# The second feed-forward layer of two tiles as a Strassen product, with blocks of two tiles that reach across batches

## The chip, the cores and the metric

The kernel runs on one core of a Trainium2 chip. The core has five engines that run side by side and wait for each other by semaphores: TensorE (matmul; in the profile PE, its weight loads PEld), VectorE (DVE), ScalarE (ACT), GpSimd (POOL) and SyncE (SP), whose queue issues nearly all of the DMA transfers. Each engine works through its instructions in the order in which the program wrote them. The metric is the device time in microseconds of one execution. The kernel before took a median of 1633.8 us in three runs (1633.7 to 1633.95).

## The reference

The computation has two stages. The first is attention in which each query keeps only its 32 largest scores; the second is a feed-forward layer with an ELU between two matrix products. All of it is in float32 on the chip (the weights arrive as float64 and are turned into float32 by the kernel).

```python
B, H, S, D = (8, 8, 576, 64)
scores = q @ k.transpose(0, 1, 3, 2) / sqrt(D)
kth = np.partition(scores, -32, axis=-1)[..., -32:-31]
scores = np.where(scores >= kth, scores, -1e9)
attn = exp(scores - max); attn /= sum(attn) + 1e-9
x = (attn @ v).transpose(0, 2, 1, 3).reshape(4608, 512)
h = x @ w_in                       # 512 x 2048
g = np.where(h > 0, h, exp(min(h, 0)) - 1)
out = g @ w_out                    # 2048 x 512
```

## The kernel before

**Tiles and steps.** Each batch has 576 queries: four tiles of 128 and a remainder of 64. The remainders of two batches, an even one and the odd one behind it, share one tile, so there are 36 tiles of 128 tokens for the feed-forward layer. A step is one tile and one pair of heads; there are 144 steps, 18 for each batch (`steps`, lines 578 to 616). Within a batch the tiles go in groups: (0,1), (2,3) and the remainder (first in odd batches, last in even ones); batch 0 takes its tiles singly.

**What a step does.** The main loop (lines 681 to 713) is software-pipelined over four steps. At step n it writes down: the score matmuls of step n+2 (`scores`, line 320), whose results ScalarE copies to `sc`; the value product of a finished group (`attend`, line 432; `avps`, its 20 matmuls run over the columns of all tiles of the group, then a ScalarE copy to `xT`); the four passes of `select` of step n on VectorE (line 342; row maxima of eight at a time and their replacement); the two halves of `mask` of step n-1 (line 367: a tiny subtraction on GpSimd, the gap, then two ScalarE activations, the second the exponential); the transposes of step n-2 on TensorE (`turn`, line 407); and `normalise` of step n-1 on GpSimd (line 390: five tiny operations and two over 576 columns). Batch 0 and 1 also carry the decoding of the weights.

**The feed-forward layer.** When a block (one, two or three tiles) has all its attention, `ffn_pieces` (line 499) appends its work to the list `ffn`. A piece `hidden(f)` (line 504) multiplies 128 of the 2048 inner columns: 4 matmuls for which the weights are a slice of `w_in` and the moving operand is `xT` of all tiles of the block (256 columns for two tiles, 384 for three). ScalarE takes the positive and the negative part out of the accumulator and applies the exponential; the last addition, a gate (`close_gates`, line 483), goes to GpSimd, in the early steps and the last block to VectorE. The result, `gT`, lies in two tiles of 8 inner blocks each. A piece `project(s, part)` (line 545) is a quarter of the second layer of one tile s: 4 matmuls with a 128x128 slice of `gT` as weights and 512 columns of `w_out` as moving operand. After the fourth part ScalarE copies the sum to `osb` and SyncE stores it. In this float32 kernel the profile shows each matmul as two instructions.

**The order.** The order on TensorE, VectorE, ScalarE and GpSimd is written out by hand (`manual_schedule`). Four times a step, `feed` (line 639) decides how many pieces are written there. It has a price for each piece (`HIDDEN`, `PROJECT`, lines 20 and 21) and a list `due` that says by which step how much work must be placed, so that each block's work is spread evenly until the next block is ready. What is left after the last step is written at the end, in one go (line 714).

**Transfers.** `load_halves` (line 223) loads one pair of heads of k and q in 8 transfers, `load_v` (line 255) loads v; the table `plan` (line 629) says how many steps ahead of the batch. All of them, and the output stores, go through SyncE's queue.

## Time and profile before

| | us |
|---|---|
| median of three runs | 1633.8 |
| the profiled execution, device time | 1633.17 |
| its span, first to last instruction | 1631.4 |
| TensorE busy (8276 matmuls) | 1569.5 |
| VectorE busy | 1454.4 |
| ScalarE busy | 1174.6 |
| GpSimd busy | 711.6 |
| TensorE in the second layer (line 551) | 522.5 |
| TensorE in the first layer (line 523) | 542.9 |

The mean granted TensorE clock was 0.988. In the lines of the profile, `ops` is the accumulator of the second layer, `hps` that of the first, `scps` the scores, `eps` the transposes and `avps` the value product. `L551` is line 551 of the kernel. A group's line gives: line, engine, operation, output <- inputs, shapes, count | busy us, mean ns of one | idle time of the engine before them and what ended it. A busy TensorE counts a matmul from its start to its modelled end, so that neighbours overlap; the chain of work that ended last gives the time from one start to the next.

### The profile page before, as it was taken

The page shows a single profiled execution, that of the slowest core. Times are in us where ns is not written, and L with a number is a line of the kernel's source. Part 1 is how long each engine was busy: PE and PEld are TensorE (multiplying, and loading weights), DVE is VectorE, ACT ScalarE, POOL GpSimd, SP SyncE. Part 2 cuts the span into 40 slices and gives each one's busy share as a digit, 9 for nine tenths or more (in the row PEclk, how much of TensorE's full clock was granted, in tenths as well). Part 3 has the DMA queues.
Part 4 walks back from the last instruction along what each step waited for, and adds up shares of the span by engine and source line. Part 5 has one row for each costly group of instructions (what it writes and reads, how often), then busy time and mean ns, then how long its engine had stood idle before and what let it go on. Part 6 is the DMA issues. An engine that isn't in the chain of part 4 may idle for free.

```text
span 1631.4 us, 25301 instructions
## 1 busy us (share of the span) xinstructions
PE 1569.5 (96%) x8276; PEld 1004.7 (62%) x8276; DVE 1454.4 (89%) x2980; ACT 1174.6 (72%) x2369; POOL 711.6 (44%) x1535
## 2 busy tenths in 40 slices
PE   4789999999999999999999999999999999999999
PEld 2477666766665757555566666655557575755564
DVE  7899999999999999999999699999999599998000
ACT  6987777877776868778577786868668695958521
POOL 4983345444443444444344443535435353534300
PEclk9779999999999999999999999999999999999999
DMA  8521310012100310022000200012100201000000
GB/s 243 187 79 36 65 37 1 7 22 45 43 1 19 54 37 7 7 40 46 23 8 15 55 21 25 1 28 45 36 14 1 43 1 36 1 13 1 7 14 13
DMA packets 188035, 56.17 MB, mean 34 GB/s; under 512 B 178176, under 2 KB 179200, under 8 KB 187904
## 3 DMA queue, kind: packets, MB, share of 16 engines
q1 hardware_dynamic: 186704, 54.26, 14.1%
q8 instruction: 66, 1.08, 0.3%
q14 instruction: 65, 0.53, 0.1%
q10 hardware_dynamic: 1200, 0.30, 0.1%
HBM read 45.09 MB, written 9.44 MB: 33 GB/s over the span
## 4 chain that ended last, share of the span: by engine, by line
PE 74%; ACT 14%; DVE 5%; POOL 3%; issue 1%; SPq 1%; DMA 1%; ACTq 0%; DVEq 0%; POOLq 0%
PE ops L551 29%; PE hps L523 22%; PE avps L448 10%; PE scps L329 7%; PE eps L422 5%; ACT sc L386 3%; DVE wk L356 2%; ACT sc L385 2%; ACT et L423 2%; DVE m L363 2%; ACT n L542 1%; ACT n L533 1%; ACT n L538 1%; ACT gT L536 1%; POOL sc L403 1%
## 5 line engine op out<-in xcount | busy, mean ns | idle before, releaser
L363 DVE MAX8 m<-wk 128x8 f32<-128x576 f32 x864 | 611.2, 751 | 0.3 <-POOL den L384 0.3
L523 PE MATMUL hps<-xT,w_in 128*128 128x256 f32 (+2 forms) x2432 | 542.9, 373 | 0.0
L551 PE MATMUL ops<-w_out,gT 128*128 128x512 f32 x1152 | 522.5, 598 | 0.0
L523 PEld LDWEIGHTS hps<-xT,w_in 128*128 128x128 f32 x2432 | 404.9, 192 | 97.4 <-issue 25.4
L356 DVE MATCH_REPLACE8 wk<-m,wk 128x576 f32<-128x576 f32 x576 | 424.5, 747 | 0.0
L551 PEld LDWEIGHTS ops<-w_out,gT 128*128 128x128 f32 x1152 | 208.6, 190 | 231.7 <-issue 230.6
L396 POOL TENSOR_SCALAR dene<-den 128x2 f32<-128x2 f32 x144 | 32.5, 225 | 693.1 <-ACT sc L386 692.5
L386 ACT ACTIVATE sc<-sc,den 128x576 f32<-128x576 f32 x288 | 223.4, 776 | 66.1 <-POOL den L384 44.4
L385 ACT ACTIVATE sc<-sc,m 128x576 f32<-128x576 f32 x288 | 225.0, 781 | 9.6 <-DVE m L363 9.5
L337 ACT ACTIVATE sc<-scps 128x576 f32<-128x576 f32 x288 | 170.9, 646 | 77.8 <-PE scps L329 77.8
L448 PE MATMUL avps<-et,vT 128*64 128x256 f32 (+2 forms) x2080 | 205.6, 328 | 20.1 <-ACT et L423 19.7
L329 PE MATMUL scps<-kqT 64*128 64x288 f32 (+1 forms) x1280 | 199.9, 443 | 25.1 <-ACT kqT L305 12.6
L349 DVE MAX8 m<-sc 128x8 f32<-128x576 f32 x288 | 202.6, 747 | 20.6 <-ACT sc L337 20.6
L403 POOL TENSOR_SCALAR sc<-sc,rec 128x576 f32<-128x576 f32 x288 | 213.5, 751 | 14.9
L423 ACT COPY et<-eps 128x512 f32<-128x512 f32 x288 | 164.6, 571 | 66.2 <-PE eps L422 66.2
L356 DVE MATCH_REPLACE8 wk<-m,sc 128x576 f32<-128x576 f32 x288 | 212.2, 746 | 0.0
L448 PEld LDWEIGHTS avps<-et,vT 128*64 128x64 f32 x2080 | 128.0, 141 | 101.0 <-ACT et L423 34.2
L422 PEld LDWEIGHTS eps<-ident,sc 128*128 128x128 f32 x1152 | 143.4, 143 | 72.4 <-issue 53.9
L493 POOL TENSOR_TENSOR gT<-n,gT 128x512 f32<-128x512 f32 (+1 forms) x120 | 166.2, 1385 | 38.0 <-ACT n L542 38.0
L422 PE MATMUL eps<-ident,sc 128*128 128x128 f32 x1152 | 174.1, 277 | 0.1
L329 PEld LDWEIGHTS scps<-kqT 64*128 64x128 f32 (+1 forms) x1280 | 107.0, 182 | 102.5 <-issue 46.2
L533 ACT ACTIVATE n<-hps 128x512 f32<-128x512 f32 (+1 forms) x156 | 87.0, 558 | 58.0 <-PE hps L523 57.1
(45 smaller groups left out, 988.5 us busy)
## 6 DMA issues: line engine op xcount, KB each, us to landing
raw<-in_moe_w_in_dram SPq DMA_DIRECT2D x16, 512.0 KB, 4.9
vT<-in_v_dram SPq DMA_DIRECT2D x64, 128.0 KB, 2.4
raw<-in_moe_w_out_dram SPq DMA_DIRECT2D x16, 512.0 KB, 3.8
out_dram<-osb SPq DMA_DIRECT2D x32, 256.0 KB, 2.0
kin<-in_k_dram SPq DMA_DIRECT2D x112, 72.0 KB, 2.4
qin<-in_q_dram SPq DMA_DIRECT2D x112, 72.0 KB, 2.5
kin<-in_k_dram SPq DMA_DIRECT2D x8, 128.0 KB, 4.7
vT<-in_v_dram SPq DMA_DIRECT2D x64, 16.0 KB, 2.2
```

Source lines behind the costliest of these rows:

```text
L329: nc.tensor.matmul(wide[i][rows, half, 0:HS], kq[part, q0 : q0 + u.t.ql], kq[part, k0 : k0 + HS], start=True, stop=True,)
L349: nc.vector.max(found[i], cur[i])
L356: nc.vector.match_replace(wk[i], found[i], cur[i], TAKEN)
L363: nc.vector.max(found[i], cur[i])
L385: nc.scalar.activation(sc, sc, AF.Prelu, scale=-1.0, bias=low, alpha=1.0 / STEEP)
L386: nc.scalar.activation(sc, sc, AF.Exp, scale=-STEEP, bias=gap, accum_out=u.den[:, i : i + 1])
L403: nc.gpsimd.tensor_scalar(u.sc[:, i, :], u.sc[:, i, :], rec[:, i : i + 1], 1.0, ALU.mult, ALU.mult)
L422: nc.tensor.transpose(ps[:, c * P : (c + 1) * P], sc[:, c0 : c0 + P], ident[:])
L423: nc.scalar.copy(g.et[:, chunks, u.at, :], ps[:, 0 : n * P].rearrange("p (c q) -> p c q", c=n),)
L448: nc.tensor.matmul(ps[i * D : (i + 1) * D, cols], vt[:, 2 * J + i if c == J else i * J + c, :], w, start=(c == 0), stop=(c == J),)
L523: nc.tensor.matmul(blk.h[:, f % bank, :], w_in[:, i, f * P : (f + 1) * P], blk.xT[:, i, 0:n_tok], start=(i == 0), stop=(i == NC - 1),)
L551: nc.tensor.matmul(blk.o[:], blk.gT[f // NG][:, f % NG, s * P : (s + 1) * P], w_out[:, f, :], start=(f == 0), stop=(f == NF - 1),)
```

## The change

The second layer of a block of two tiles is the product of a 256 x 2048 matrix with a 2048 x 512 one. Cut into halves in each direction, with a11, a12, a21, a22 for the quarters of `gT` (tile, half of the inner columns) and b11 to b22 for those of `w_out`, it is eight products of quarters. The changed kernel forms it with seven, in Winograd's form of Strassen's scheme:

- four differences of quarters of `w_out` (t1 = b12 - b11, t2 = b22 - t1, t4 = b21 - t2, t3 = b22 - b12) are made once, on GpSimd, in four steps at the start of batch 1 (`differences`), and stored to DRAM (`scratch`), in 16 pieces. They are read back for each block through six buffers of 256 KB, four pieces for each of the four products that use them (`stream`, on SyncE's queue, issued when the piece before has been used);
- four sums of quarters of `gT` per block are made in place by GpSimd, 128 x 1024 elements each, between the products;
- each product is 8 matmuls over 256 columns; ScalarE copies its result out, and seven sums of 128 x 256 on GpSimd put the four quarters of the output together. The two output tiles are stored after products 5 and 6.

Blocks of three tiles are gone. The first five blocks are single tiles, then the tiles in the order in which they finish are taken two by two, across batches; one single tile remains at the end. So that a pair always finishes together, batches 3, 4 and 7 go through their tiles as (0), (1,2), (3). With the first group of a batch single, batch 4 has its own loading plan. `xT` of the early single blocks has two buffers instead of three, the output tile two instead of one, and the price list of the planner counts seven products.

```diff
-HIDDEN = {1: 1.1, 2: 1.85, 3: 2.7}
+HIDDEN = {1: 1.1, 2: 1.85}
...
-    T = 3 * P
+    T = 2 * P
+    W = dm // 2
+    TF, TB = 2, 6
+    QT = NG // TF
...
-    xpool = pool("x", 3)
-    opool = pool("o", 1)
+    xpool = pool("x", 2)
+    opool = pool("o", 2)
+    scratch = pool("scratch", 1, space=bass.MemoryType.DRAM)
...
+        late["e"] = ctx.enter_context(tc.tile_pool(name="e", bufs=2))
+        late["t"] = ctx.enter_context(tc.tile_pool(name="t", bufs=TB))
...
+        def quarter(s, h):
+            return blk.gT[h][:, :, s * P : (s + 1) * P]
+
+        def combine(dst, x, y, op):
+            nc.gpsimd.tensor_tensor(dst, x, y, op)
+
+        def emit(s):
+            for t in blk.tiles[s]:
+                p0 = t.cols.start - s * P
+                nc.sync.dma_start(out[t.rows, :], blk.o[s][p0 : p0 + t.ql, :])
+
+        def product(j):
+            left, right = slice(0, W), slice(W, dm)
+            while blk.after:
+                blk.after.pop(0)()
+            if j == 7:
+                return
+            if j == 0:
+                close_gates(upto=(blk.number, NF - 1))
+                blk.o = [opool.tile([P, dm], FP32, tag="osb", name="osb") for _ in range(2)]
+                blk.e = [late["e"].tile([P, W], FP32, tag="e", name="e") for _ in range(2)]
+            a11, a12 = quarter(0, 0), quarter(0, 1)
+            a21, a22 = quarter(1, 0), quarter(1, 1)
+            c11, c12 = blk.o[0][:, left], blk.o[0][:, right]
+            c21, c22 = blk.o[1][:, left], blk.o[1][:, right]
+            e0, e1 = blk.e[0][:], blk.e[1][:]
+            x, name, dst, after = (
+                (a11, "b11", c11, [(a21, a21, a22, ALU.add)]),
+                (a12, "b21", c12, [(a11, a21, a11, ALU.subtract)]),
+                (a21, "t1", c22, [(a12, a12, a11, ALU.subtract)]),
+                (a22, "t4", e0, [(a21, a22, a11, ALU.subtract)]),
+                (a11, "t2", c21, [(c21, c21, c11, ALU.add), (c11, c11, c12, ALU.add)]),
+                (a12, "b22", c12, [(c12, c12, c21, ALU.add), (c12, c12, c22, ALU.add)]),
+                (a21, "t3", e1, [
+                    (c21, c21, e1, ALU.add), (c22, c22, c21, ALU.add),
+                    (c21, c21, e0, ALU.add),
+                ]),
+            )[j]
+            if j == 0:
+                combine(*after.pop())
+            sums = ps_f.tile([P, dm], FP32, tag="f", name="ops")[:, left]
+            for f in range(NG):
+                if name[0] == "b":
+                    w = w_out[:, NG * (name[1] == "2") + f, right if name[2] == "2" else left]
+                else:
+                    if f % TF == 0:
+                        t = streamed.pop(0)
+                    w = t[:, f % TF, :]
+                nc.tensor.matmul(sums, x[:, f, :], w, start=f == 0, stop=f == NG - 1)
+                if name[0] == "t" and f % TF == TF - 1:
+                    stream()
+            if 0 < j < 4:
+                combine(*after.pop())
+            nc.scalar.copy(dst, sums)
+            blk.after += [lambda x=x: combine(*x) for x in after]
+            if j > 4:
+                blk.after.append(lambda: emit(j - 5))
...
+        if blk.slots == 2:
+            return layer + [
+                (PROJECT * (j < 7), behind, lambda j=j: product(j), blk.number)
+                for j in range(8)
+            ]
...
+    def stream():
+        k = ahead_of[0]
+        ahead_of[0] += 1
+        if k >= 4 * QT * sum(x.slots == 2 for x in blocks):
+            return
+        t = late["t"].tile([P, TF, W], FP32, tag="t", name="tw")
+        src = kept[names[k // QT % 4], k % QT]
+        nc.sync.dma_start(t[:], src[:].rearrange("p (f n) -> p f n", f=TF))
+        streamed.append(t)
...
+    def differences(q):
...
+        for name, x, y in (
+            ("t1", b12, b11), ("t2", b22, "t1"), ("t4", b21, "t2"), ("t3", b22, b12),
+        ):
+            t = late["t"].tile([P, TF, W], FP32, tag="t", name="tw")
...
+            nc.gpsimd.tensor_tensor(t[:], x, y, ALU.subtract)
...
+            nc.sync.dma_start(
+                kept[name, q][:].rearrange("p (f n) -> p f n", f=TF), t[:]
+            )
...
     for b in range(B):
-        if b % 2 == 0:
...
+        if b == 0:
+            order = [(0,), (1,), (2,), (3,)]
+        elif (len(ends) + b % 2 - J - 1) % 2 == 0:
+            order = [(0, 1), (2, 3)]
+        else:
+            order = [(0,), (1, 2), (3,)]
...
+    while ends:
+        n = 1 if len(blocks) <= J else 2
+        blk = Block(len(blocks), len(ends[:n]))
...
-        total += NF * HIDDEN[blk.slots] + 4 * blk.slots * PROJECT
+        total += NF * HIDDEN[blk.slots] + (4 if blk.slots == 1 else 7) * PROJECT
...
+        if len(orders[b][0]) == 1:
+            plan = ((7, 5, 2), (5, 3, 0), (3, 1, -1), (2, 0, -2))
         if b % 2 == 1:
             plan = ((7, 5, 0), (6, 4, -2), (5, 3, -3), (4, 3, -3))
...
+    for x in range(QT):
+        at(first[1] - 2 + 2 * x, differences, x)
+    for _ in range(TB):
+        at(first[1] - 2 + 2 * QT, stream)
```

More of the change, by code (lines that the diff above doesn't have):

```diff
@@ L44, in __init__ @@
         self.xT = None
-        self.gT = []
+        self.gT, self.after = [], []
         self.left = 0
@@ L516, in hidden @@
                 else:
-                    n = late["f"].tile([P, 2 * T], FP32, tag="n", name="n")
+                    n = late["f"].tile([P, 4 * P], FP32, tag="n", name="n")
                 blk.n = n[:, 0 : unit * n_tok].rearrange("p (f t) -> p f t", f=unit)
@@ L565, in ffn_pieces @@
         part = HIDDEN[blk.slots]
         behind = 2 * NF if blk.number else 0
-        return [
+        layer = [
             (part, max(behind, NC * (f // 4 + 1)), lambda f=f: hidden(f), blk.number)
             for f in range(NF)
-        ] + [
+        ]
[3 more added lines that the diff above has]
+                for j in range(8)
+            ]
+        return layer + [
             (PROJECT, max(behind, NF + (part + 1) * NF // 4),
@@ L575, in ffn_pieces @@
         ]
+    streamed, ahead_of = [], [0]
+    names = ("t1", "t4", "t2", "t3")
+    def stream():
[7 more added lines that the diff above has]
+        streamed.append(t)
+    kept = {}
+    def differences(q):
+        fs = slice(q * TF, (q + 1) * TF)
+        low = slice(NG + q * TF, NG + (q + 1) * TF)
+        b11, b12 = w_out[:, fs, 0:W], w_out[:, fs, W:dm]
+        b21, b22 = w_out[:, low, 0:W], w_out[:, low, W:dm]
+        made = {}
+        for name, x, y in (
+            ("t1", b12, b11), ("t2", b22, "t1"), ("t4", b21, "t2"), ("t3", b22, b12),
+        ):
+            t = late["t"].tile([P, TF, W], FP32, tag="t", name="tw")
+            made[name] = t
+            y = made[y][:] if isinstance(y, str) else y
+            nc.gpsimd.tensor_tensor(t[:], x, y, ALU.subtract)
+            kept[name, q] = scratch.tile([P, TF * W], FP32, tag=f"{name}{q}", name="kept")
+            nc.sync.dma_start(
+                kept[name, q][:].rearrange("p (f n) -> p f n", f=TF), t[:]
+            )
     ffn = []
@@ L579 @@
     blocks, tight = [], 2 * NHP
+    orders, ends, division = [], [], []
     for b in range(B):
-        if b % 2 == 0:
-            rest = 2 * J
-            division = [(0,), (1,), (2,), (3,), (rest,), (4, 5), (6, 7)]
-            if b > 0:
-                division = [(0, 1), (2, 3), (rest, 4, 5), (6, 7)]
-            slots = {}
-            for part in division:
-                blk = Block(len(blocks), len(part))
-                blocks.append(blk)
-                slots.update((x, (blk, s)) for s, x in enumerate(part))
+        if b == 0:
[4 more added lines that the diff above has]
+            order = [(0,), (1, 2), (3,)]
+        orders.append([(J,)] + order if b % 2 else order + [(J,)])
+        ends += [(b, qt) for qts in orders[b] for qt in qts if qt < J or b % 2]
+    while ends:
+        n = 1 if len(blocks) <= J else 2
+        blk = Block(len(blocks), len(ends[:n]))
+        blocks.append(blk)
+        division += [(x, (blk, s)) for s, x in enumerate(ends[:n])]
+        del ends[:n]
+    slots = dict(division)
+    for b in range(B):
         first[b] = len(steps)
@@ L595 @@
             if qt == J:
-                (blk, slot), c0, n = slots[rest], (b % 2) * R, R
+                (blk, slot), c0, n = slots[b | 1, J], (b % 2) * R, R
                 rows = slice(r0, r0 + R)
             else:
-                (blk, slot), c0, n = slots[(b % 2) * J + qt], 0, P
+                (blk, slot), c0, n = slots[b, qt], 0, P
                 rows = slice(r0, r0 + J * (P - 1) + 1, J) if b == 0 else slice(r0, r0 + P)
@@ L605 @@
             tiles.append(t)
-        order = [(0, 1), (2, 3), (J,)] if b % 2 == 0 else [(J,), (0, 1), (2, 3)]
-        if b == 0:
-            order[:2] = [(0,), (1,), (2,), (3,)]
-        for qts in order:
+        for qts in orders[b]:
             for hp in range(NHP // 2 if qts == (J,) else NHP):
```

## The prediction

> **What bounds the kernel now.** I read the page's first part, then the stretches of one batch each, then the chain at the end, then the groups by shape, then the waits.
>
> ```profile
> PE 1569.5 (96%) x8276; PEld 1004.7 (62%) x8276; DVE 1454.4 (89%) x2980; ACT 1174.6 (72%) x2369; POOL 711.6 (44%) x1535
> ```
>
> TensorE is busy for all but 62 us of the span. VectorE comes next with 177 us to spare, so a second look by stage is needed. I cut the span where VectorE starts the first row maximum of each batch (stretch, its length, busy PE, PEld, DVE, ACT, POOL, clock, DMA share, GB/s):
>
> ```profile
> 218.30:395.80 177.50, 172.30 (x1089) 118.89 (x1088) 177.50 (x367) 138.64 (x281) 83.32 (x188) 1.00 0.12 25
> ...
> 578.70:756.20 177.50, 175.19 (x939) 107.82 (x938) 177.50 (x367) 132.00 (x269) 77.23 (x178) 1.00 0.13 27
> 756.20:953.00 196.80, 196.25 (x965) 123.41 (x963) 180.25 (x372) 145.54 (x292) 83.99 (x192) 1.00 0.13 26
> ...
> 1130.50:1332.40 201.90, 201.35 (x987) 126.13 (x985) 180.61 (x371) 150.19 (x304) 86.18 (x194) 1.00 0.09 19
> ...
> 1510.80:1631.40 120.60, 116.51 (x407) 67.31 (x405) 5.63 (x9) 38.97 (x78) 18.19 (x37) 1.00 0.04 11
> ```
>
> Batches 1 and 3 last exactly as long as VectorE needs, 177.5 us, with TensorE 2 to 5 us short of full. In batches 4 and 6 VectorE idles 16 to 21 us and TensorE about 0.5. Then come 120.6 us of nearly TensorE alone. So VectorE sets a floor of 177.5 us a batch and TensorE, slightly above it, sets the time. The chain at the end, in order of time (start, us, what):
>
> ```profile
> 1572.46 27.63 PE hps L523 x128
> 1600.09 27.48 PE ops L551 x64
> 1627.64 0.58 ACT osb L560
> ```
>
> These are clean prices, back to back: a matmul instruction over 256 columns takes 27.63/128 = 0.2159 us, one over 512 takes 27.48/64 = 0.4294 us. Half the width costs half the time to within 0.6%. The groups by shape and the waits (waiter, releaser, us in total, times, longest):
>
> ```profile
> L551 PE MATMUL ops<-w_out,gT 128*128 128x512 f32 x1152 | 522.5, 598 | 0.0
> ...
> L523 PE MATMUL hps<-xT,w_in 128*128 128x384 f32 x384 | 131.8, 490 | 0.0
> ...
> L493 POOL TENSOR_TENSOR gT<-n,gT 128x512 f32<-128x512 f32 x96 | 122.6, 1277 | 20.1 <-ACT n L542 20.1
> ...
> L493 POOL TENSOR_TENSOR gT<-n,gT 128x768 f32<-128x768 f32 x24 | 43.7, 1819 | 17.9 <-ACT n L542 17.9
> ```
>
> ```profile
> POOL dene L396 <- ACT sc L386: 692.5, 138, 10.8
> ...
> ACT sc L386 <- POOL den L384: 44.4, 49, 4.3
> ```
>
> and of SyncE's own queue:
>
> ```profile
> SPq L563 <- ACT osb L560: 608.0, 28, 75.0
> SPq L229 <- DVE kqT L283: 433.2, 26, 56.6
> ```
>
> GpSimd spends its idle time waiting for the exponential; SyncE's queue reaches its transfers tens of microseconds early. After the first loads no line of the waits has TensorE waiting for a transfer.
>
> **The change part by part.**
>
> *Second layer of a pair.* Before, two tiles x 16 blocks x 2 instructions = 64 instructions of 512 columns, 27.48 us. After, 7 products x 8 x 2 = 112 instructions of 256 columns, 112 x 0.2159 = 24.18 us. There are 15 pairs after (30 tiles), so 15 x 3.30 = 49.5 us of TensorE go. The seven start-ups for eight give at most 0.19 us a pair more (the ops group of 8 takes 3.44 us after a transpose, 3.63 after other work). The products have the shape of the first layer's pair matmuls, one 128x128 weight load for each, so that the row of 0.2159 holds for them. A page of the Trainium skill, "Perfetto Trace Analysis" (Identifying the Most-Contended Engine), would have headroom judged by the share of weight loading and not by matmul busy time, and this change adds 720 weight loads at the row's 190 ns, 137 us, which takes PEld from 62% to about 72%. By that rule the change eats headroom, and if the loads added all their time the sum would end at 1594 + 137 = 1731. The row of 256 columns, which already has one load per matmul, runs at column speed, so I put the loads at nothing.
>
> *First layer, divided anew.* Before: 5 single blocks, 11 pairs, 3 triples; after: 6 singles, 15 pairs. Four pairs more are 4 x 27.63 = 110.5 us; one single, 128 instructions at 2.78/24 = 0.116 us, is 14.8; three triples less, 3 x 128 x 2.58/8 = 123.8. Sum +1.5 us.
>
> *Attention groups.* Batches 3, 4 and 7 go in the order (0),(1,2),(3): 24 single groups for 12 pairs. A pair's 20 value matmuls take 2.31 us in the chain; a single's took 1.41 from start to the next group's start (212.82 to 214.23). 24 x 1.41 - 12 x 2.31 = +6.1 us. The scores and transposes are per tile and stay.
>
> *ScalarE* copies 7 x 256 columns a pair for 2 x 512: 105 x 0.37 + 6 x 0.59 against 36 x 0.59 is +21 us on 1175, spread. Each copy makes ScalarE wait for TensorE and the masks queue behind it, but the first layer does the same every two pieces (3.45 us), with four operations of 0.6 us instead of one, and TensorE has no gap there. Cost nothing; without that cover a mask is late by at most one product.
>
> *GpSimd* gets, a pair, four sums of 1024 columns and seven of 256. From 1277 ns for 512 and 1819 for 768 (542 ns per 256) that is 4 x 2.36 + 7 x 0.73 = 14.6 us, by straight doubling 4 x 2.55 + 7 x 0.64 = 14.7; 220 us in all, plus 16 weight differences x 1.28 = 20. 711 becomes about 950, 59%. In the product phase it is denser: a pair's FFN fills eight steps by the planner's costs (54.45 in 8 steps), the products 3.65 of them, so 4 us a step on top of 3.4 (normalise with its small operations and the two gaps), in a step of 10. The order gives each sum time: the sum for product 2 is issued before product 0, those for products 4, 5, 6 after products 1, 2, 3, so two whole products, 6.9 us, lie between issue and use, and it takes 2.4 to 2.55. What is queued behind: the gaps (ScalarE's exponential waits), then normalise, for whose result TensorE's transposes wait a step later; a sum delays them by 2.6 us at most, against a 1.28 us gate in the same place now. The one tight place is the start: product 0 closes all gates, and product 1 reads the last. The chain is ScalarE 0.59+0.59+0.63+0.63 and GpSimd 1.28 = 3.7 us against 3.45 for product 0: 0.3 us a pair if nothing lies between. I take +2 us for all of GpSimd; the bounds are 0 and, if every product phase waits once for an exponential (692.5/138 = 5.0 us), 15 x 5.0 = 75.
>
> VectorE beside a busier GpSimd: its maxima take 715 to 760 ns everywhere, and its step 9.64 us, whether GpSimd was busy 17 or 27 of 50 us. "SBUF — State Buffer" (Who interferes with whom) in the Trainium skill speaks against the change: VectorE and GpSimd share a port pair as an exclusive lock, when VectorE has two inputs or a two-port mode. If the 240 us were all locked, VectorE would need 1454 + 240 = 1694 us, an estimate from that page's rule. The rows show no such lock on these instructions, so I add nothing.
>
> *SyncE and the transfers.* The stream adds 15 x 16 loads of 256 KB (63 MB) and 16 stores. The nearest row is the 256 KB output, 0.36 us to issue and 2.0 to land. Six buffers are used up in 6 x 0.86 = 5.2 us of uninterrupted product, so 2.8 us are left over each time. A load waits for the matmuls that free its buffer, and the outputs wait for GpSimd's last sums; behind both stand the k, q and v loads, which until now were issued tens of microseconds early. They are taken at least one step (10 us) after their issue and land in 2.4 us. The other way, a batch's four pairs of k/q loads hold the queue 4 us each. If all 28 met a product phase (3.65 of 8 steps) and overran the 2.8 us, that is 28 x 0.46 x 1.2 = 15 us, the upper bound; below, 0. I take 0. Where TensorE's work is late, next in line are these loads.
>
> *Buffers.* xT's two instead of three: the planner finishes a block's first layer (steps 8, 13, 18) before the next but one takes its first columns (11, 15, 19), so nothing waits.
>
> *The end.* The last block is one tile, not two: 14.8 + 13.7 us for 55.1 after the last attention; this is part of the TensorE sum already, and moves load from the tail into the batches.
>
> **Sum.** -49.5 + 1.5 + 6.1 + 2 = -40 us. Per batch, counting the planner's pieces at these prices, TensorE's load was 170, 176, 182, 186, 192, 186, 209 us in batches 1 to 7 and 91 behind; it becomes 174, 180, 186, 180, 184, 180, 195 and 70. Only batch 1 stays under VectorE's 177.5, so that almost all of the gain is felt. The profiled execution took 1633.17 us (span 1631.4), 0.6 below the median of 1633.8: 1633.2 - 40 = 1593, 1594 as a median.
>
> **The rivals.**
> - *VectorE paces the middle.* The new loads are within 1 to 9 us of 177.5 a batch, and uneven steps may make TensorE wait. Then the batches keep their length and only the tail shrinks, by 55.1 - 28.5 = 27 us: 1607. Against it: in batches 4 to 7 VectorE waits today, 45 us over its floor in total.
> - *The stream is late*, by its bound of 15 us or somewhat more: 1609 to 1625. For it: SyncE is one queue with waits of 57 us for VectorE's transposes in it. Against it: those waits are for work that lies earlier in the written order.
> - *GpSimd is late (slower).* A sum behind a normalise that waits for the exponential holds up a product. It decides from 40/15 = 2.7 us a pair; at 5.0 us a pair, 1594 + 73 = 1667; at 3.5 us about 1645. For it: 138 such waits, up to 10.8 us. Against it: two products lie between.
> - *The products do not run at 256-column speed*: at 0.2454 us (0.2159 x 1.137) an instruction the saving is zero and 1641 remains. The first layer speaks against it.
>
> **How the numbers follow.** Forecast 1594 (own range 1583 to 1604): 0.62. VectorE's pace, 1607: 0.15. Stream late, 1609 to 1625: 0.10. GpSimd late beyond the point: 0.09. Products slow: 0.04, half of it within 0.2%. A measurement here tells 0.2%, 3.3 us. Faster 0.87, same 0.03, slower 0.10. Low end 1583: the singles at half a pair's price (-6), nothing for GpSimd (-2), and fewer start-ups (-3). High end 1622: it takes in VectorE's pace and most of a late stream.
>
> **What would show it.** In the profile after: 1680 ops instructions of 256 columns at 0.216 in the chain, 7 x 3.45 us a pair; PE busy near 1530; the last stretch near 100 us; no new line of TensorE waiting for GpSimd's sums or for the stream above 5 us in all; maxima still 0.75 us. Wrong it would be if TensorE waits for a quarter's sum or a streamed tile in each pair, or if stretches of 177.5 us appear in all batches.

## The result: slower by 48 us

The changed kernel takes a median of 1681.7 us (1680.14 to 1681.81) against 1633.75 us for the kernel before in the same comparison: a ratio of 1.0293, interval 1.0275 to 1.0311. The forecast was 1594, so its sign was wrong. The profiled execution took 1681.76 us, its span is 1679.7 us, the mean granted clock of TensorE 0.978 (0.988 before).

The first part of the page after, engine by engine (busy us, share of the span, instructions):

```profile
PE 1561.8 (93%) x9492; PEld 1206.1 (72%) x9492; DVE 1456.7 (87%) x2976; ACT 1191.3 (71%) x2460; POOL 955.6 (57%) x1732
```

TensorE's busy time fell by only 7.7 us, and its idle time rose from 62 us (1631.4 - 1569.5) to 118 (1679.7 - 1561.8), by 56: together the 48 us. No engine is busier than 93%, and none but TensorE is above 87%. Averages don't show what became the limit. The groups of the second layer and of VectorE's maxima, after:

```profile
L619 PE MATMUL ops<-tw,gT 128*128 128x256 f32 x960 | 221.5, 384 | 0.6 <-POOL gT L575 0.6
L619 PE MATMUL ops<-w_out,gT 128*128 128x256 f32 x720 | 164.5, 381 | 0.0
L575 POOL TENSOR_TENSOR gT<-gT 128x1024 f32<-128x1024 f32 x60 | 141.8, 2365 | 2.1 <-PE ops L619 0.8
L369 DVE MAX8 m<-wk 128x8 f32<-128x576 f32 x864 | 610.9, 747 | 18.8 <-POOL den L390 18.8
```

With 87.4 us for the single tiles left, the second layer is 473.4 us busy instead of 522.5: the 49 us that the forecast counted are there. The other matmuls take them back: the first layer is busy 553.8 us instead of 542.9, the scores 210.7 instead of 199.9 and the value product 228.8 instead of 205.6, 45 us more where the forecast had 7.6. The lower clock can account for at most some 17 us of that (an estimate: 0.010 of 1680 us). The products wait 0.6 us for sums and nothing for the streamed pieces. The stretches of a batch each, cut as before (length, busy PE, PEld, DVE, ACT, POOL, clock, DMA share, GB/s; batches 1, 3, 4, 6, and the tail):

```profile
218.80:403.60 184.80, 174.93 (x1099) 123.80 (x1100) 177.91 (x367) 130.65 (x267) 92.58 (x189) 0.97 0.20 52
...
604.50:795.20 190.70, 180.46 (x1135) 143.34 (x1134) 178.43 (x368) 133.08 (x280) 109.20 (x205) 0.97 0.27 70
795.20:1009.10 213.90, 201.46 (x1245) 160.44 (x1244) 181.06 (x371) 157.38 (x327) 121.02 (x223) 0.99 0.30 74
...
1191.50:1405.10 213.60, 205.53 (x1154) 159.05 (x1151) 181.23 (x372) 151.79 (x314) 124.84 (x224) 0.99 0.26 73
...
1574.60:1679.70 105.10, 100.92 (x579) 81.75 (x577) 12.51 (x25) 47.37 (x99) 42.38 (x60) 1.00 0.17 55
```

The tail shrank as forecast, but batches 1, 3, 4 and 6 are 7, 13, 17 and 12 us longer than before. Batch 2, not shown, grows most, by 18 us (182.9 to 200.9), and batch 5 by 5. In batch 4 neither TensorE (201.5 of 213.9) nor VectorE (181.1) is full any more. The waits after (waiter, releaser, us in total, times, longest):

```profile
POOL dene L402 <- ACT sc L392: 435.4, 125, 10.8
...
PEld avps L454 <- ACT et L429: 90.0, 64, 3.0
ACT sc L392 <- POOL den L390: 89.3, 41, 5.6
...
PE avps L454 <- ACT et L429: 67.7, 60, 2.8
...
ACT osb L624 <- PE ops L619: 61.0, 31, 4.6
ACT osb L624 <- POOL osb L575: 59.8, 13, 4.6
```

TensorE's value product waits for `et`, the copy by which ScalarE brings the transposed weights out of the accumulator: 67.7 us. The same wait before:

```profile
PE avps L448 <- ACT et L423: 19.7, 26, 2.4
```

ScalarE's exponential (line 392) waits for the gap on GpSimd: 89.3 us, against 44.4. The last two lines are the copies of the seven products: ScalarE waits for the product, and, in a line with no counterpart before, for GpSimd's sums. The chain's shares say the same:

```profile
PE 49%; ACT 33%; POOL 10%; issue 3%; DVE 3%; DMA 1%; SPq 0%; ACTq 0%; POOLq 0%; DVEq 0%
```

Before they were:

```profile
PE 74%; ACT 14%; DVE 5%; POOL 3%; issue 1%; SPq 1%; DMA 1%; ACTq 0%; DVEq 0%; POOLq 0%
```

Two pieces of the chain of after show the two ways in which ScalarE gets onto it. First, a stretch with first-layer work in it (start, us, what):

```profile
1248.06 0.60 ACT n L539
1248.66 0.49 ACT gT L542
1249.15 0.53 ACT n L544
...
1251.09 0.87 ACT sc L392 x2
1251.95 0.64 ACT et L429 x2
...
1255.75 0.63 ACT n L548
1256.38 0.48 ACT et L429
...
1256.90 2.37 PE avps L454 x18
```

From 1248.06 to 1256.86 ScalarE works without a gap, and the value product waits for the last of it. Its work for a step is, at this chain's durations, two mask halves (2 x 1.55), the copies `et` (0.64 + 0.48), two score copies (2 x 0.65 by their group) and half an `xT` copy (0.16), 5.7 us. Two first-layer units are 4.4 more (2.25 + 2.13, of which the last addition, line 548, is 0.63 each). That is 10.1 us, for a step that VectorE needs only 9.86 for (177.5/18). In a step with two units ScalarE has no time to spare, though its mean is 71%. Over a whole first-layer phase it isn't full, however. Here are one such phase of the kernel before and the phase of after from which this piece of the chain is taken (columns as in the stretches above):

```profile
1213.80:1256.40 42.60, 42.60 (x242) 33.61 (x241) 38.22 (x80) 39.12 (x80) 21.84 (x43) 1.00 0.02 7
1242.60:1289.80 47.20, 44.68 (x251) 34.38 (x249) 45.54 (x95) 40.42 (x83) 24.05 (x49) 1.00 0.12 37
```

ScalarE is busy for 92% of the first and 86% of the second; TensorE for all of the first and 95% of the second. After the change the two wait for each other in turn: TensorE's value product waits until 1256.90 for the last copy, and ScalarE, two score copies later, waits 1.37 us for the value product. Second, the start of a product phase:

```profile
1206.34 2.47 POOL gT L499 x2
...
1208.89 2.36 POOL gT L575
1211.24 0.16 POOL den L390
...
1211.43 0.87 ACT sc L392 x2
...
1215.37 2.37 PE avps L454 x18
```

GpSimd closes two gates, forms a quarter's sum (2.36 us) and only then the gap, an operation of 0.16 us for which the exponential, the copy and the value product stand in line.

### The profile page after: what moved, and what is told of

It reads as the page before. It is cut to its first block, busy times and chain, and to the rows that moved or that the text cites. A ratio compares the mean times of both kernels' runs of the same rounds, so it can differ in the third digit from the quotient of the medians.

```text
span 1679.7 us, 28505 instructions
## 1 busy us (share of the span) xinstructions
PE 1561.8 (93%) x9492; PEld 1206.1 (72%) x9492; DVE 1456.7 (87%) x2976; ACT 1191.3 (71%) x2460; POOL 955.6 (57%) x1732
## 4 chain that ended last, share of the span: by engine, by line
PE 49%; ACT 33%; POOL 10%; issue 3%; DVE 3%; DMA 1%; SPq 0%; ACTq 0%; POOLq 0%; DVEq 0%
PE ops L619 17%; PE hps L529 11%; PE avps L454 10%; ACT sc L392 8%; ACT sc L391 5%; ACT et L429 5%; ACT n L548 4%; PE scps L335 4%; ACT n L539 3%; ACT n L544 3%; PE ops L557 3%; ACT gT L542 3%; PE eps L428 3%; POOL gT L499 2%; POOL gT L575 2%
## 5 line engine op out<-in xcount | busy, mean ns | idle before, releaser
L529 PE MATMUL hps<-xT,w_in 128*128 128x256 f32 (+1 forms) x2688 | 553.8, 356 | 0.0
L529 PEld LDWEIGHTS hps<-xT,w_in 128*128 128x128 f32 x2688 | 447.2, 194 | 64.0 <-issue 21.5
L392 ACT ACTIVATE sc<-sc,den 128x576 f32<-128x576 f32 x288 | 223.5, 776 | 112.6 <-POOL den L390 89.3
L454 PE MATMUL avps<-et,vT 128*64 128x256 f32 (+2 forms) x2320 | 228.8, 322 | 67.7 <-ACT et L429 67.7
L454 PEld LDWEIGHTS avps<-et,vT 128*64 128x64 f32 x2320 | 145.3, 147 | 157.8 <-ACT et L429 90.0
L499 POOL TENSOR_TENSOR gT<-n,gT 128x512 f32<-128x512 f32 x136 | 173.1, 1277 | 123.4 <-ACT n L548 123.4
L335 PE MATMUL scps<-kqT 64*128 64x288 f32 (+1 forms) x1280 | 210.7, 444 | 34.1 <-ACT et L429 19.8
L619 PE MATMUL ops<-tw,gT 128*128 128x256 f32 x960 | 221.5, 384 | 0.6 <-POOL gT L575 0.6
L619 PEld LDWEIGHTS ops<-tw,gT 128*128 128x128 f32 x960 | 177.6, 190 | 36.2 <-issue 8.8
L335 PEld LDWEIGHTS scps<-kqT 64*128 64x128 f32 (+1 forms) x1280 | 111.5, 182 | 106.3 <-issue 35.6
L619 PE MATMUL ops<-w_out,gT 128*128 128x256 f32 x720 | 164.5, 381 | 0.0
```

The source lines that it names most:

```text
L335: nc.tensor.matmul(wide[i][rows, half, 0:HS], kq[part, q0 : q0 + u.t.ql], kq[part, k0 : k0 + HS], start=True, stop=True,)
L392: nc.scalar.activation(sc, sc, AF.Exp, scale=-STEEP, bias=gap, accum_out=u.den[:, i : i + 1])
L454: nc.tensor.matmul(ps[i * D : (i + 1) * D, cols], vt[:, 2 * J + i if c == J else i * J + c, :], w, start=(c == 0), stop=(c == J),)
L499: nc.gpsimd.tensor_tensor(dst, n, dst, ALU.add)
L529: nc.tensor.matmul(blk.h[:, f % bank, :], w_in[:, i, f * P : (f + 1) * P], blk.xT[:, i, 0:n_tok], start=(i == 0), stop=(i == NC - 1),)
L619: nc.tensor.matmul(sums, x[:, f, :], w, start=f == 0, stop=f == NG - 1)
```

## The experiments

Theory A: ScalarE is short of time in first-layer phases, and the product phases, in which it used to catch up, are now shorter and fuller of waits. Theory B: what counts is GpSimd, by the gap's place behind the sums, by the sums' buffers, or by the weight differences. Theory C: the transfers. Theory D: the new division and order of tiles, without any product. Comparisons are with runs of the kernel before on the same chip (medians 1632.87 to 1633.92).

**The division alone.** The tiles and the order of after, the second layer of before.

```diff
-        if blk.slots == 2:
-            return layer + [
-                (PROJECT * (j < 7), behind, lambda j=j: product(j), blk.number)
...
-        total += NF * HIDDEN[blk.slots] + (4 if blk.slots == 1 else 7) * PROJECT
+        total += NF * HIDDEN[blk.slots] + 4 * blk.slots * PROJECT
...
-    for x in range(QT):
-        at(first[1] - 2 + 2 * x, differences, x)
-    for _ in range(TB):
-        at(first[1] - 2 + 2 * QT, stream)
```

> The blocks and the order of tiles of the changed kernel, but the second layer as before: eight quarter projections of 512 columns per pair, no sums, no stream. If the loss comes from the sums and copies of the seven products (theory 1, ScalarE's queue), this is the kernel before plus 1.5 us of first layer and 6 us of single attention groups: 1634 to 1645. If the new division and order are at fault (theory 2), 1665 or more, and TensorE waits for the et copies here too.

1661.28 us, ratio 1.0172 (1.0157 to 1.0187), between the two times that were expected: the division costs 28 us where the forecast had 7.6, more than half of the loss without a single product. Its chain:

```profile
PE 67%; ACT 23%; DVE 5%; POOL 2%; issue 1%; DMA 1%; SPq 0%; ACTq 0%; DVEq 0%; POOLq 0%
```

ScalarE has 23% of it, GpSimd 2%; the value product waits 48.4 us for `et`, 28.7 more than before, about as much as the time lost. On top of it the products bring not the -47.5 us of the forecast (-49.5 and +2) but +20.

**The products alone.** The division and order of before, its eleven pairs in seven products with their sums and copies, but without differences and stream (each product takes a quarter of `w_out`).

```diff
-                    if f % TF == 0:
-                        t = streamed.pop(0)
-                    w = t[:, f % TF, :]
+                    w = w_out[:, f, left]
...
-        total += NF * HIDDEN[blk.slots] + (4 if blk.slots == 1 else 7) * PROJECT
+        total += NF * HIDDEN[blk.slots] + (7 if blk.slots == 2 else 4 * blk.slots) * PROJECT
```

> Division and order of the kernel before (11 pairs, 3 triples), the pairs' second layer in seven products with sums and copies, without differences and stream (products use quarters of w_out; the output is not the reference's). TensorE's load falls by 11 x 3.3 = 36 us: 1597 if the products cost nothing else. If the sums cost here what they cost in the changed kernel (27 us for 15 pairs, 20 for 11): 1617. If the new division was needed for the loss: below 1605. Above 1633: the products lose by themselves.

1644.22 us (1640.4 to 1648.01), ratio 1.0059 (1.0042 to 1.0076). Eleven pairs at 3.30 us less are 36 us of TensorE's work gone, and the kernel is 10 us slower: the products lose their gain without the new division too.

**No stream and no differences**, in the changed kernel.

```diff
-                    if f % TF == 0:
-                        t = streamed.pop(0)
-                    w = t[:, f % TF, :]
+                    w = w_out[:, f, left]
...
-                if name[0] == "t" and f % TF == TF - 1:
-                    stream()
...
-    for x in range(QT):
-        at(first[1] - 2 + 2 * x, differences, x)
-    for _ in range(TB):
-        at(first[1] - 2 + 2 * QT, stream)
```

> The changed kernel with all products on quarters of w_out itself: no differences made, nothing stored, nothing streamed (the output is not the reference's). Theory 3, the transfers on SyncE's queue hold something up: the time falls by 15 us or more. Theory 1: 1675 to 1682, since no line of the waits has TensorE waiting for a streamed tile.

1666.22 us in two runs, ratio 1.0204 (1.0183 to 1.0224): 15 us of the 48. All of it lies in batches 1 and 2 (184.8 and 200.9 us become 177.5 and 192.3); the other stretches agree within 0.1 us. So it is what happens once, not what happens in each pair.

**Differences only**: made and stored, never read back.

```diff
-                    if f % TF == 0:
-                        t = streamed.pop(0)
-                    w = t[:, f % TF, :]
+                    w = w_out[:, f, left]
...
-                if name[0] == "t" and f % TF == TF - 1:
-                    stream()
...
-    for _ in range(TB):
-        at(first[1] - 2 + 2 * QT, stream)
```

> The changed kernel with the 16 weight differences made and stored as it does, but never read back: the products use quarters of w_out (the output is not the reference's). Without differences and stream it took 1666, with both 1681.7. If the differences cost the 15 us: 1678 to 1683, and batch 1 is 7 us longer than 177.5 again. If the stream costs them: 1664 to 1668.

1680.97 us, ratio 1.0288 (1.0271 to 1.0305), as the changed kernel. The 15 us belong to the sixteen differences, made and stored; reading the 63 MB of stream costs nothing that shows there (0.7 us). Theory C falls. The chain of the changed kernel at one such place: from 220.07 us on GpSimd makes four differences, of which the last two are shown here with the gate and the exponential behind them:

```profile
222.73 2.51 POOL tw L676 x2
225.25 1.24 POOL gT L499
...
226.66 0.87 ACT sc L392 x2
```

**No sums**: neither the quarters' nor the outputs' are formed, everything else as in after.

```diff
-                combine(*after.pop())
+                after.pop()
...
-            blk.after += [lambda x=x: combine(*x) for x in after]
```

> The changed kernel without any sum on GpSimd, neither the four of 1024 columns nor the seven of 256 (the output is not the reference's: the products use the raw quarters and are not put together). Seven products, their ScalarE copies and the stream stay. Theory 1 with GpSimd as its cause: the 42 us that were forecast appear, 1590 to 1605. If ScalarE's seven copies, each of which waits for TensorE, are the cause: still above 1650. Theory 2: above 1650.

1654.63 us, ratio 1.0135 (1.012 to 1.015): the sums cost 27 us, where the forecast had 2 for all of GpSimd. They aren't all of the loss: 21 us remain without them, and the 1590 to 1605 of sums alone at fault were not reached.

**The gap earlier on GpSimd**: the same tiny subtraction, written right behind `normalise` of the step before, ahead of the sums that follow.

```diff
-        else:
-            nc.gpsimd.tensor_tensor(gap, low, top, ALU.subtract)
...
+    def gaps(u):
+        u.den = small.tile([P, 4], FP32, tag="den", name="den")
+        for i in range(2):
+            nc.gpsimd.tensor_tensor(
+                u.den[:, 2 + i : 3 + i], u.last[:, i, 7:8], u.first[:, i, 0:1],
+                ALU.subtract,
+            )
...
             normalise(prev)
+        if cur and n >= tight:
+            gaps(cur)
```

> The changed kernel with the two gap subtractions written on GpSimd a step earlier, right behind normalise and ahead of the sums (same engine, same work). Theory A with the gap behind the sums as one cause (89 us of ScalarE waiting for it): 10 to 30 us less, 1652 to 1672. If GpSimd now waits for VectorE with normalise behind it: 1680 or more.

1650.1 us, ratio 1.0099 (1.0084 to 1.0114): 31.6 us back with no work removed, slightly more than the 10 to 30 expected. The wait of the exponential for the gap, 89.3 us in after, is now

```profile
ACT sc L391 <- POOL den L399: 13.5, 13, 1.8
```

So it is less the 14.6 us a pair of GpSimd's time that cost, than the place of 0.16 us of it in the queue. Theory B holds in this form.

**The gap on VectorE**, at the end of the row maxima.

```diff
+            if r == TOP_K // 8 - 2 and not more:
+                u.den, u.gapped = small.tile([P, 4], FP32, tag="den", name="den"), True
+                for i in range(2):
+                    nc.vector.tensor_tensor(
+                        u.den[:, 2 + i : 3 + i], u.last[:, i, 7:8],
+                        u.first[:, i, 0:1], ALU.subtract,
+                    )
...
-        else:
+        elif not u.gapped:
             nc.gpsimd.tensor_tensor(gap, low, top, ALU.subtract)
```

> The changed kernel with the gap (128x1 subtraction ahead of the exponential) at the end of the row selection on VectorE instead of in GpSimd's queue, behind the sums. Theory 1 by the gap: ScalarE's 89 us of waiting for the gap go, and 40 to 90 us of the time with them, 1590 to 1640. If the wait only moves (ScalarE then waits for the product's copy or GpSimd's normalise is late instead): 1665 or more.

1660.57 us, ratio 1.0165 (1.0148 to 1.0182), 21 us less than after and between the two times expected. VectorE's busy time rises by 53 us to 1509.8 (272 more instructions, 0.19 us each), and its share of the chain from 3% to 49%: part of what GpSimd's queue no longer costs goes to a new bound.

**A buffer of its own for product 5.** Product 5's copy goes into `c12`, which GpSimd must first have read for `c11 += c12`; here it gets a third small tile.

```diff
-            e0, e1 = blk.e[0][:], blk.e[1][:]
+            e0, e1, e2 = (x[:] for x in blk.e)
...
-                (a12, "b22", c12, [(c12, c12, c21, ALU.add), (c12, c12, c22, ALU.add)]),
+                (a12, "b22", e2, [(c12, e2, c21, ALU.add), (c12, c12, c22, ALU.add)]),
```

> The changed kernel with a buffer of its own for product 5, so that ScalarE's copy no longer waits until GpSimd has read the old content of c12 (60 us of ScalarE waiting for GpSimd, 13 times, up to 4.6). Theory A (ScalarE's queue sets the time): 5 to 25 us less, 1657 to 1677. If the wait was covered: 1680.

1677.25 us, ratio 1.0267 (1.0252 to 1.0282): 4.5 us less, and hardly that for certain, as the interval of the changed kernel begins at 1.0275. ScalarE's new wait for GpSimd is 59.8 us long in after. So most of that wait cost nothing.

**ScalarE relieved, in three kernels.** Left out is the last addition of first-layer units on ScalarE (line 548 after, 542 before), so that the values lack their -1: some 80 us of ScalarE's busy time, taken from the changed kernel, from the division alone, and from the kernel before as a control.

```diff
                 if apart:
-                    nc.scalar.activation(blk.n, blk.n, AF.Copy, bias=-1.0)
```

> The changed kernel without ScalarE's fourth operation per two pieces of the first layer, the copy with bias -1 (630 ns, 136 times, 86 us; the output is not the reference's). Theory A, in the first-layer phases ScalarE is the engine that is full (its 5.8 us of attention a step and two times 2.2 us of the first layer make 10.2), so that the et copies come late for TensorE's value products: 1682 falls by 20 to 60, to 1622 to 1662, and TensorE's waits for et in these phases (48 us) fall below 15. Theory B, ScalarE is late only because it waits for others (TensorE's products, GpSimd's gaps): 1672 to 1682.

> The same removal in the kernel with the new division and the old second layer (1661). Theory A: 1630 to 1645, nearly the 1640 that TensorE's load would give. Theory B: 1655 to 1661.

> The same removal in the kernel before, as a control. There TensorE's load sets the time and its waits for et are 9 us in these phases: both theories 1622 to 1634.

| | with it | without it | gain |
|---|---|---|---|
| the changed kernel | 1681.7 | 1612.99, ratio 0.9873 (0.9858 to 0.9887) | 69 |
| the division alone | 1661.28 | 1612.35, ratio 0.9874 (0.9859 to 0.9889) | 49 |
| the kernel before | 1633.81 | 1613.24, ratio 0.9877 (0.9862 to 0.9892) | 21 |

Three kernels that differ by 48 us end within 1 us of each other, the first two lower than even theory A had them (1622 and 1630 at the least). This much of theory A holds: ScalarE's work in the first-layer phases lies on the path that sets the time, for 0.63 us less of it, 136 times, gives back 69 us in the changed kernel. That the three meet is partly chance, for the changed kernel still has its sums, its differences and its late gaps (82.8 us of the exponential's waiting), and the shorter products against them. Nor is ScalarE asked for much more work: it is busy 1174.6 us before, 1181.3 in the division alone and 1191.3 in the changed kernel. What differs is when that work comes, between ScalarE's waits and TensorE's. In the changed kernel the value product's wait shrinks from 67.7 us to

```profile
PE avps L454 <- ACT et L429: 25.8, 29, 1.9
```

The control missed what was expected of it. It gained 21 us although TensorE was busy for all but 0.5 us of batches 4 and 6: ScalarE already cost that much in the kernel before, and little idle time of TensorE showed it. Most of it lay inside TensorE's busy time: at the same mean clock of 0.988 the same 8276 matmuls are busy 1569.5 us with the addition and 1554.8 without it. GpSimd's gates wait less too (123.4 to 80.2 us in the changed kernel), so that the gain isn't all ScalarE's time.

**The addition replaced, in the kernel before.** Adding -1 to every element of g adds the same row, minus the column sums of `w_out`, to every row of the output. GpSimd adds up the 16 slices of `w_out` in batch 0, one matmul with a matrix of -1 gives the row, and GpSimd adds it to each output tile.

```diff
-                if apart:
-                    nc.scalar.activation(blk.n, blk.n, AF.Copy, bias=-1.0)
...
+        nc.gpsimd.tensor_tensor(late["shift"][:], first, w_out[:, f, :], ALU.add)
...
+        nc.tensor.matmul(ps[:], minus[:, 0:P], shift[:], start=True, stop=True)
+        nc.scalar.copy(shift[:], ps[:])
...
+                        nc.gpsimd.tensor_tensor(o[:], o[:], late["shift"][:], ALU.add)
```

> The kernel before with the constant row in place of ScalarE's copy with bias -1 (36 sums of 512 columns on GpSimd, 46 us in all, behind the output copy). The control without the copy and without the row took 1613: 1611 to 1620 if the row hides on GpSimd, above 1625 if its waits hold up normalise.

1623.12 us, ratio 0.9935 (0.992 to 0.995): half of the 21 us as a kernel that computes everything, and 3 us above the range that was expected if the row hides on GpSimd.

**The same row in the division alone.**

> The new division and order with the old second layer, and the constant row in place of ScalarE's copy with bias -1. Without the copy and without the row it took 1612. Theory A: 1612 to 1622, so that the division costs nothing once ScalarE has room, and what the mended kernel (1605) lies below is the worth of the seven products. If the division has a cost of its own: above 1630.

1617.13 us, ratio 0.9898 (0.9882 to 0.9915): 6 us below the kernel before with the row. Together with the table (1612.35 against 1613.24) it says that the division costs nothing once this addition is off ScalarE's queue. Theory D, as a cost of the division itself, falls. The 28 us are what it costs with the addition there.

**All mended together**: the row (half of it added in the products' places), the early gap, the own buffer, and the differences spread, one a step. With the row in memory the stream has five buffers instead of six.

```diff
-        at(first[1] - 2 + 2 * x, differences, x)
+        for y in range(4):
+            spread.setdefault(first[1] + 4 * x + y, []).append((differences, (x, y)))
...
+            if 0 < j < 4:
+                half = late["shift"][:, right if j == 2 else left]
+                blk.after.append(lambda: combine(dst, dst, half, ALU.add))
```

> The changed kernel with everything that was found: ScalarE's copy with bias -1 replaced by one constant row (the negative column sums of w_out), which GpSimd adds to the outputs (three sums of 256 columns a pair, one of 512 for a single); own buffer for product 5; gaps early; the 16 weight differences one a step instead of four every second step; five streamed buffers. From 1613 (the kernel without that copy) less 5 to 15 for the differences and 10 to 30 for the other two: 1570 to 1600. TensorE's load puts the floor near 1590 to 1595 by the forecast's sum, VectorE's near 1540. If ScalarE's lateness comes back through GpSimd's added work: above 1613.

1604.58 us, ratio 0.9824 (0.9807 to 0.984): faster than both kernels, though above the 1570 to 1600 that was expected. The trace shows new waits of TensorE, 9.4 us for GpSimd to fill the matrix of -1, and 10.3 us for streamed pieces.

**Mended again**: the matrix filled early, the differences three steps sooner.

```diff
-            spread.setdefault(first[1] + 4 * x + y, []).append((differences, (x, y)))
+            spread.setdefault(first[1] - 3 + 4 * x + y, []).append((differences, (x, y)))
...
-    at(19, total_row)
+    at(20, total_row)
```

> The mended kernel with two waits of TensorE taken out that its own additions had made: the matrix of minus ones for the constant row is written eight steps earlier (9.4 us of TensorE waiting for GpSimd), and the weight differences and the first streamed loads start three and two steps earlier (6.8 us of waiting for the first streamed piece). 1605 less 10 to 16: 1589 to 1596, which is the forecast of 1594 with ScalarE out of the way. If the waits only move: 1600 or more.

1602.56 us, ratio 0.9811 (0.9796 to 0.9826), 79 us under the changed kernel and the lowest median of all; the intervals of the three mended kernels overlap, so that it can't be called better than the other two. Of the 10 to 16 us expected it gained 2. Its streamed products, by the groups:

```profile
L649 PE MATMUL ops<-tw,gT 128*128 128x256 f32 x960 | 224.9, 387 | 17.4 <-DMA tw<-kept 17.4
```

Against the division with the row (1617.13) the products now gain 14.6 us. The instruction time saved is there, 48 us from start to start, but TensorE's gaps rise by 29 us over the span and its other matmuls take 4 us more. Of the gaps, 17.4 us are the wait for streamed pieces, 14.3 at one place, 416 us, where the first piece stands behind a load of k in SyncE's queue. The other 12 are the value product's wait for `et`, 23.8 us against 11.9.

**Mended a third time**: two differences a step, so that the stream can start sooner.

```diff
-            spread.setdefault(first[1] - 3 + 4 * x + y, []).append((differences, (x, y)))
+            spread.setdefault(first[1] - 2 + 2 * x + y // 2, []).append((differences, (x, y)))
...
-        at(first[1] - 2 + 4 * QT, stream)
+        at(first[1] - 2 + 2 * QT, stream)
```

> The mended kernel again, with the weight differences two a step behind normalise, from step 16, and the first streamed loads at step 24 as in the changed kernel, so that they stand ahead of the loads of k and q of the next batch, behind which they waited (14.3 us of TensorE waiting for the first streamed piece, at 416 us). 1603 less 12 to 16: 1587 to 1591. If the differences, closer together, cost that again: 1598 or more.

1604.74 us, ratio 0.9823 (0.9808 to 0.9837), not the 12 to 16 us less that was expected, and no different from the run before within the intervals. The wait for pieces fell to 11.3 us, but batch 1 lengthened from 177.5 to 179.3, with denser differences in it: the wait seems to have moved rather than gone.

## Why the prediction was wrong, point by point

- **The second layer, -49.5 us: right as instruction time**, 522.5 to 473.4 us busy. Products ran at the speed of 256 columns, and a weight load for each cost nothing that the groups show. What failed is the step from there to the time ("almost all of the gain is felt"): the time that TensorE no longer needed was not TensorE's to give back. The sign "PE busy near 1530" was missed as well, with 1561.8.
- **ScalarE, "Cost nothing": the step that failed.** Its reason was that "the first layer does the same every two pieces" and "TensorE has no gap there". The absence of a gap was read as room on ScalarE. Its work in a step with two first-layer units, 10.1 us by the chain, could have been added up from rows of before. The runs showed instead that ScalarE's work there sets the time: its share of the chain rose from 14 to 33%, TensorE's wait for `et` from 19.7 to 67.7 us, and without the additions 69 us come back in the changed kernel, 21 before. What the seven copies have in it is argued only. The old second layer of a pair was 27.5 us with two copies; the new one is 24.2 us with seven, which wait 121 us in all for their products and for GpSimd. But with product 5 in a buffer of its own most of the wait for GpSimd cost nothing, and no run takes the copies alone away.
- **GpSimd, "+2 us", bounds 0 and 75: mis-sized.** The durations were right (2.365 and 0.73 us for 2.36 and 0.73). The sums cost 27 us, the gap's place behind them 31.6; these overlap and don't add. That "a sum delays them by 2.6 us at most" was true of each, but it was judged against the gate in the same place, while gate and sum now stand there one behind the other.
- **The sixteen differences, counted in GpSimd's load (20 us) and within its +2: 15 us.** They come four at a time, 5 us in a row, ahead of the gap, in a batch whose TensorE had 5 us to spare.
- **The division, +7.6 us: 28 measured, nothing with the addition off ScalarE.** Counting TensorE's instructions couldn't show it. Which part of it makes ScalarE later, the order of single groups or the pairs in place of triples, stays open: ScalarE's busy time is only 6.7 us longer, and the new division in the old order was not tried.
- **SyncE and the stream, 0: right in the changed kernel**, as the run with the differences only shows. It comes back as a wait of TensorE where other waits were taken away: 6.5 us with the gap early, 13.7 with the gap on VectorE, 17.4 in the mended kernel.
- **VectorE beside a busier GpSimd: right.** The maxima take 747 ns with GpSimd at 57%, and 749 in the mended kernel with GpSimd at 63%. *Buffers of xT: nothing*, and no wait appeared. But one buffer was missed, `c12`; it costs some 4 us.
- **The end: right**, 105 us against "near 100".
- **The rivals.** "GpSimd is late" had the sign and one of the engines, but another place: there the sum holds up a product, and products waited 0.6 us. In the trace it holds up the gap, which the working had named as "what is queued behind" and then priced by one sum. No rival had ScalarE. What would show the prediction wrong was therefore incomplete as well: neither of its two signs appeared, while TensorE waited for `et`. *VectorE paces the middle* has its share only once ScalarE is relieved: batches 1, 3 and 5 of the mended kernel last 177.5 us each, VectorE's floor.

Of the 48 us: the division brought 28 and the rest of the change 20, in which the differences are 15 and the sums 27 us, against a saving of which 22 us would be felt if these parts added up. They were measured by taking each away from a kernel in which the others remain, though, and as they load the same engines, another order would give other parts.

The mended kernel stays 9 us above the forecast, with 29 us more of gaps than its counterpart; how much of the 9 is the first streamed piece, how much VectorE's floor, and how much the copies, was not settled.

## What to carry to other kernels

Add up an in-order engine's work step by step before you call its share of the span room: here an engine at 72% had 10.1 us of work in a step of 9.86. It need not be full to set the time. ScalarE was busy 86 to 92% of the two first-layer phases shown, and 0.63 us less in each unit still gave 69 us, because TensorE waited for what stood behind it in the queue. A tiny operation for which another engine waits belongs ahead of long ones in its queue; moving it cost nothing and gave 31.6 us. A control, the suspected cost taken out of the kernel before as well, told more than any single ablation of the changed kernel.

## What the runs showed of the hardware

TensorE's granted clock fell where TensorE was held up for 2 us or less. From 200 to 250 us, around the start of batch 1 (length, then as above), in the changed kernel:

```profile
200.00:250.00 50.00, 44.65 (x314) 31.04 (x313) 47.85 (x100) 31.01 (x64) 28.14 (x53) 0.90 0.30 75
```

and without differences and stream:

```profile
200.00:250.00 50.00, 46.77 (x407) 34.00 (x406) 50.00 (x106) 37.70 (x78) 22.85 (x57) 1.00 0.19 41
```

In the first, a pause of 1.89 us that ends at 218.8 us is followed by 5 us without a gap at a clock of 0.75 (220 to 225 us), and at 234.68 us, at a clock of 0.88, 8 instructions of 512 columns take 4.38 us (3.44 at full clock). There a stall costs more than its length. The total of the pauses doesn't decide, for 3.2 us of them in the second leave the clock at 1.00; what does was not tried. The Trainium skill, "TensorE: Matmul & The Clock Gate" (Part 1), has the clock halved after an idle window of about 3.4 us. In this stretch no idle time of TensorE reaches that, and the clock fell all the same, so the measurement decides here.

The same skill's "Perfetto Trace Analysis" (Identifying the Most-Contended Engine) says that matmul busy time is no good measure of how near a kernel is to its limit. The prediction set it against a row and left its warning at that. The control agrees with the warning: 21 us were to be had in a kernel whose TensorE showed 96% busy, and almost 100% in batches 4 and 6. Of the measures that it gives instead, the share of weight loading would have spoken against the products, and the runs don't bear that out: in the mended kernel it is 75%, and 16 instructions of 256 columns of a product take 3.46 us from start to start, 0.216 us each as before.
